# T3 of the down projection from seven inner products, spread among T2, T1 and B22

## The chip, the cores and the metric

The kernel runs on one core of a Trainium2 chip. A core has TensorE (PE, matrix products into PSUM), VectorE (DVE) and ScalarE (ACT) for elementwise work, GpSimd (POOL) and SyncE (SP), which here mostly issue DMAs. Each engine works through its own list of instructions in order, and waits on semaphores for the others. The metric is the device time of one execution in microseconds (us).

## What is computed

```python
x = A_x                                             # 2048 tokens, 640 wide
g = sigmoid((x * gate_w).sum(-1, keepdims=True))
q, k, v = split(x @ wqkv)                           # 32 heads of 20
pq, pk = phi(q), phi(k)                             # phi(t) = where(t > 0, t + 1, exp(t)) + 1e-6
kv, z = einsum("bhsd,bhse->bhde", pk, v), pk.sum over tokens
a = (pq @ kv) / (pq @ z + 1e-6) @ wo
h = sigmoid(x @ w_gate) * (x @ w_up)                # 1536 wide
b = h @ w_down
out = g * a + (1 - g) * b
```

All inputs and the output are float32.

## The kernel before

**Precision.** Each float32 operand is split into a high part (an ACT copy to fp32r) and a low part (a DVE subtraction), by `split`. One product of 128x128 by 128x512 is then three matmuls (`mm3`: high x high, high x low, low x high), written on lines 203 and 205.

**Stages.** The first 300 us or so compute k, the small matrix that k and v make with wo, and q; then twelve steps over the 1536 features compute h, and the attention's scaled pq is prepared on DVE beside them. Both end as rows of one long contraction. The last stage, the down projection, starts near 510 us and contracts this against w_down and the attention's matrix. It is this stage that the change rewrites.

**The down projection.** The 2048 tokens are two pairs (pr = 1 and 0) of two groups of 512 (g0, g1). The contraction has 16 blocks of 128, of which w_down's twelve and the attention's first four form pairs (even, odd), p = 0 to 7; the attention's fifth block is the "rest" (`hr`, `wl`). The output's 640 columns are five blocks of 128; four of them form two pairs (q = 0, 1), the fifth is accumulated apart, in a PSUM tile `rot`. So each pr is a 2x2 by 2x2 block product and is computed by seven products, named B11, B21, T1, T2, T3, T4 and B22 after the form of h that goes in. The forms of h are built by DVE while h is computed, and stored by POOL in DRAM as `h_dram[pr, name]`, one tile of 8 x 512 columns for each (h1T3 is form T3 of pair 1). The weights' forms are E (plain, even blocks), O (plain, odd blocks), SE and SO (sums, built by `load_s` and `sum_s` from line 1510 and kept in `s_dram`), and L for the rest.

A *pass* (class `Pass`) is one form of one pair: four h pieces (pp = 0 to 3), each 128x1024 (two rows of the contraction), against the columns of q = 0, of q = 1 and, in four of the forms, of the fifth block (`EXTRA`). A piece of B11, B21, T1 or B22 thus feeds 18 matmuls, one of T2, T3 or T4 feeds 12. X holds the PSUM sums of B11, T2, T3 and, for pair 0, T4; Z those of T1 and B22; outputs leave through tiles `ot` and stores by POOL (`put`, line 1736).

**What sets the order.** `SEQ` (line 1607) lists the passes: B11 of both pairs piece by piece in turn, B21 of pair 1, T4 of pair 1, B21 of pair 0, then T2, T1, T3 and B22 of pair 1, the same of pair 0, and T4 of pair 0. `HQ` is the list of the h pieces in that order, 56 of them. PE's order follows `HQ`. The h pieces are loaded by SP into raw tiles `hw` (three of them; `load_h`), split by ACT and DVE into tiles `hf` (five of them, `NH`), and used by PE. A split of piece k is queued when piece k - 5 has been used, and the load of piece k + 3 is issued when piece k has been split. Weights come in through two raw tiles `ws` (`load_down`, `next_down`) and are split in the gaps. Where a split stands among ACT's and DVE's other work is decided when the program is built, by class `Order`: it keeps running estimates of each engine's time and takes the next item when it fits (`fill`), at the latest where PE needs it (`need`). `order.late` holds actions that are put into the program when the estimate passes a time.

DMAs of one engine are issued in its program order: where SP waits with a load for data or for a free tile, its later loads wait behind it. The same holds for POOL's stores.

Of the kernel before, what the change touches and what calls it, by code (L numbers as in the profile page):

```python
# [15 lines left out]
P = 128  # L16
# [162 lines left out]
def gated_mix_kernel(ctx: ExitStack, tc: tile.TileContext, xt, xn, wk, wv, wo, wst_q, wst_f, out_t):  # L179
# [81 lines left out]
    s_dram = [dram.tile([P, 2, TG], F32, name=f"s{p}") for p in range(FC // 2 + 2)]  # L261
# [1248 lines left out]
    def load_s(p):  # L1510
        st["in_b"] = not st["q"]
        st["st"] = st["b"][:, 0:2] if st["in_b"] else st["a"][:, 2:4]
        for j in range(2):
            nc.sync.dma_start(st["st"][:, j], raw_down(j, p // 2)[:, p % 2, :4])
        st["s"] = max(order.pe, order.vec) + 6.0

    def sum_s(p):
        e, o = (st["st"][:, j].rearrange("p (o k c) -> p k o c", k=2, c=P) for j in range(2))
        (e0, e1), (o0, o1) = ((t[:, 0], t[:, 1]) for t in (e, o))
# [4 lines left out]
        nc.gpsimd.dma_start(s_dram[p], st["st"])  # L1524
# [14 lines left out]
    hooks = {0: begin, 3: den_all}  # L1539
    NH = 5  # L1540
    WA, RAW = {}, {}

    def wd_tile(key, cols):
        pool = PL["ha"] if key == ("E", 0) else PL["wa"]
# [4 lines left out]
    def load_down(key, t=None):  # L1549
# [3 lines left out]
        if kind == "S":  # L1553
            v = t[:, :8 * P].rearrange("p (j o c) -> p j o c", j=2, c=P)
            nc.sync.dma_start(t[:, :8 * P].rearrange("p (j c) -> p j c", j=2), s_dram[n])
# [3 lines left out]
        else:  # L1559
            src = raw_down(0, n)[:, :, 0::2] if kind == "E" else raw_down(1, n)  # L1560
# [3 lines left out]
        RAW[key] = v, max(order.pe, order.vec) + (8.0 if kind == "S" else 5.0)  # L1564

    d_loads = [("E", pp) for pp in range(1, PP)] + [("O", pp) for pp in range(4)] + [("L", 0)]
    d_loads += [("S", p) for p in range(2 * PP)]

    def next_down():
        if d_loads:  # L1570
            load_down(d_loads.pop(0))

    def queue_down(key):
# [5 lines left out]
        def s_part(j):  # L1579
            t = wd_tile((("SE", "SO")[j], n // 2), 4)  # L1580
            split(t[:, 0, n % 2], t[:, 1, n % 2], RAW[key][0][:, j])
            if j:
                order.then(next_down)

        def diff():
            v = RAW[key][0]
            sub(v[:, KC:], v[:, 0:4:2], v[:, 1:4:2])

        def whole():
            if kind == "L":  # L1590
                t = WA[key] = PL["wa"].tile([P, 2, KC + 2, P], F32R, name="wl", tag="wl")
            else:
                t = wd_tile(key, 3 if kind == "E" else KC)
            split(t[:, 0], t[:, 1], RAW[key][0])
            if key != ("E", 0):
                order.then(next_down)

        if kind == "S":
            for j in range(2):
                order.add(a_cost(4 * P), v_cost(4 * P), lambda j=j: s_part(j), ("wa", ("SE", "SO")[j], n // 2), at)  # L1600
        else:
            w = {"E": 6, "O": 10, "L": 7}[kind] * P
# [4 lines left out]
    SEQ = [[(1, "B11"), (0, "B11")], [(1, "B21")], [(1, "T4")], [(0, "B21")]]  # L1607
    SEQ += [[(pr, n)] for pr in (1, 0) for n in ("T2", "T1", "T3", "B22")] + [[(0, "T4")]]
    HQ = [(pr, n, pp) for turn in SEQ for pp in range(PP) for pr, n in turn]
    HF, HR = {}, {}  # L1610

    def load_h(k, tiles=None):
        if k < len(HQ):
            pr, n, pp = HQ[k]
            if tiles:
                for i, t in enumerate(tiles):
                    nc.sync.dma_start(t, h_dram[pr, n][:, 2 * pp + i])
            else:
                tiles = PL["hb"].tile([P, 2, TG], F32, name="hw", tag="hw", bufs=3)
                nc.sync.dma_start(tiles, h_dram[pr, n][:, 2 * pp:2 * pp + 2])  # L1620
# [17 lines left out]
    REST, REST_AT = {}, {13: 0, 20: 1, 36: 0}  # L1638
# [23 lines left out]
    for f in range(FC):  # L1662
# [36 lines left out]
        if not nxt:  # L1699
            queue_h(0)  # L1700
# [41 lines left out]
    load_h(2)  # L1742
    load_h(3)
    load_h(4)
# [4 lines left out]
    plan += [("S", p) for p in range(2 * PP)]  # L1749
# [4 lines left out]
    hk = done_h = 0  # L1754

    def advance():

        while plan:
# [7 lines left out]
            else:  # L1766
                order.stream = order.mid if kind == "S" else order.items
# [184 lines left out]
```

## Time and profile before

| | us |
|---|---|
| median of 3 runs | 726.71 (726.53 to 726.83) |
| profiled execution | 727.02 |
| its span, from the first to the last instruction | 724.2 |
| PE busy in it | 719.5 |
| DVE, ACT, POOL busy | 486.3, 320.5, 128.9 |

The page gives, for one profiled execution, each engine's busy time, the chain of work that ended last, groups of instructions with their mean time, and the idle time ahead of them with what ended it ("<-ACT hf" means that the engine waited for ACT's work on tile hf). PEld is the weight load, which overlaps the matmuls. Where an action is a DMA, "SPq" or "POOLq" is the queue that issued it. Matmuls overlap too, so a matmul's length is no measure of its place in PE's time; the distance between starts is.

### The profile page before, as it was taken

To read this page: it belongs to the slowest core of one execution; us is meant where nothing else is said; L and a number is where in the kernel's file an instruction comes from. 1 tells how busy PE (TensorE), PEld (TensorE's weight loads), DVE (VectorE), ACT (ScalarE), POOL (GpSimd) and SP (SyncE) were. 2 spreads that over 40 slices of the span, in tenths; PEclk is the share of its full clock that TensorE was granted. 3 is DMA by queue.
4 is the path that set the end of the run, shared out by engine and by line. 5 is a ranking of instruction groups with operands and counts; after the bars stand their busy time and mean duration, and the time that the engine had idled before them with its cause. 6 is when DMAs were issued, how large, how long until landed. Compare 5 with 4: busy or idle time off the path is not lost.

```text
span 724.2 us, 9524 instructions
## 1 busy us (share of the span) xinstructions
PE 719.5 (99%) x3411; PEld 607.8 (84%) x3411; DVE 486.3 (67%) x773; ACT 320.5 (44%) x541; POOL 128.9 (18%) x221
## 2 busy tenths in 40 slices
PE   9999999999999999999999999999999999999997
PEld 8999998888888888888888888888888888888886
DVE  4878576868764698678879778786866664434340
ACT  6664637166756233333333232334367644424321
POOL 0311011122520023213224222330200000010000
PEclk9999999999999999999999999999999999999999
DMA  7553536897555474556578658474987975565431
GB/s 253 140 141 70 162 55 159 201 302 247 191 174 182 153 238 126 176 194 242 188 273 299 221 188 294 157 258 143 324 300 259 329 231 190 158 213 194 146 113 72
DMA packets 59491, 144.05 MB, mean 199 GB/s; under 512 B 7310, under 2 KB 20782, under 8 KB 59445
## 3 DMA queue, kind: packets, MB, share of 16 engines
q1 hardware_dynamic: 40757, 88.50, 38.4%
q0 software_dynamic: 18544, 54.83, 23.2%
q8 instruction: 26, 0.43, 0.3%
q14 instruction: 20, 0.16, 0.1%
q10 hardware_dynamic: 144, 0.13, 0.1%
HBM read 89.81 MB, written 49.84 MB: 193 GB/s over the span
## 4 chain that ended last, share of the span: by engine, by line
PE 99%; DVE 0%; ACT 0%; issue 0%
PE ch L205 18%; PE cc L205 17%; PE rot L205 16%; PE dd L205 14%; PE ch L203 9%; PE cc L203 8%; PE rot L203 8%; PE dd L203 7%; PE cc L1136 1%; PE rot L300 0%; PE cc L1216 0%; DVE ot L219 0%; ACT ot L215 0%
## 5 line engine op out<-in xcount | busy, mean ns | idle before, releaser
L219 DVE TENSOR_TENSOR hf<-hw,hf 128x1024 fp32r<-128x1024 f32 x54 | 65.8, 1223 | 68.7 <-ACT hf L215 68.4
L215 ACT ACTIVATE hf<-hw 128x1024 fp32r<-128x1024 f32 x54 | 56.8, 1057 | 53.7 <-PE rot L205 30.5
L219 DVE TENSOR_TENSOR c<-cc,c 128x512 f32<-128x512 f32 x56 | 37.7, 686 | 45.9 <-PE cc L205 40.5
L205 PE MATMUL dd<-hf,wa 128*128 128x512 f32 x160 | 49.3, 389 | 0.0
L205 PE MATMUL ch<-hf,wa 128*128 128x512 f32 x160 | 49.3, 389 | 0.0
L1736 POOL DMA_DIRECT2D out_t<-ot x18 | 9.7, 540 | 183.8 <-DVE ot L219 180.8
L215 ACT ACTIVATE wG<-wst 128x640 fp32r<-128x640 f32 x17 | 12.4, 737 | 65.0 <-PE dd L205 65.0
L215 ACT ACTIVATE c<-ch 128x512 f32<-128x512 f32 x32 | 19.1, 597 | 48.8 <-PE ch L205 44.0
L205 PE MATMUL rot<-hf,wa 128*128 128x512 f32 x128 | 39.4, 389 | 0.0
L205 PE MATMUL cc<-hf,wa 128*128 128x512 f32 x128 | 39.4, 389 | 0.0
L203 PE MATMUL dd<-xrh,wG 128*128 128x512 f32 x90 | 35.3, 393 | 0.0
L205 PEld LDWEIGHTS ch<-hf,wa 128*128 128x128 f32 x160 | 30.0, 188 | 6.3
L205 PEld LDWEIGHTS dd<-hf,wa 128*128 128x128 f32 x160 | 30.0, 188 | 6.3
L205 PE MATMUL dd<-xrh,wG 128*128 128x512 f32 x90 | 35.1, 390 | 0.0
L205 PE MATMUL dd<-xrl,wG 128*128 128x512 f32 x90 | 35.0, 389 | 0.0
L219 DVE TENSOR_TENSOR c<-c,om 128x512 f32<-128x512 f32 x48 | 33.1, 692 | 1.6
L203 PE MATMUL cc<-xbh,wS 128*128 128x512 f32 x84 | 32.7, 389 | 0.0
L205 PE MATMUL cc<-xbl,wS 128*128 128x512 f32 x84 | 32.7, 389 | 0.0
L205 PE MATMUL cc<-xbh,wS 128*128 128x512 f32 x84 | 32.7, 389 | 0.0
L203 PE MATMUL dd<-hf,wa 128*128 128x512 f32 x80 | 31.1, 389 | 0.0
L203 PE MATMUL ch<-hf,wa 128*128 128x512 f32 x80 | 31.1, 389 | 0.0
L215 ACT ACTIVATE c<-rot 128x512 f32<-128x512 f32 x24 | 14.2, 597 | 38.1 <-PE rot L205 30.8
(471 smaller groups left out, 2084.6 us busy)
## 6 DMA issues: line engine op xcount, KB each, us to landing
hf<-p_dram SPq DMA_DIRECT2D x16, 512.0 KB, 4.7
hw<-h1T SPq DMA_DIRECT2D x16, 512.0 KB, 5.4
hw<-h0T SPq DMA_DIRECT2D x16, 512.0 KB, 4.3
wst<-wst_f SPq DMA_DIRECT2D x12, 640.0 KB, 4.7
xst<-xt SPq DMA_DIRECT2D x10, 640.0 KB, 7.0
h1T<-c POOLq DMA_DIRECT2D x24, 256.0 KB, 2.7
h0T<-c POOLq DMA_DIRECT2D x24, 256.0 KB, 3.0
hw<-h1B SPq DMA_DIRECT2D x11, 512.0 KB, 4.5
```

Of the source, the lines that this page charges most:

```text
L203: nc.tensor.matmul(o, l_hi, r, start=first, stop=False, skip_group_check=True)
L205: nc.tensor.matmul(out, a, b, start=False, stop=last and n == 1, skip_group_check=True)
L215: nc.scalar.activation(out, src, fn, **kw)
L219: nc.vector.tensor_tensor(out, a, b, op=op)
L1136: nc.tensor.matmul(ps[:w, b0:b1], v[:, m, :w], g(m), start=(m == 0), stop=(m == KC - 1))
L1736: (eng or nc.gpsimd).dma_start(out_t[o * P:(o + 1) * P, g * TG + c0:g * TG + c1], t[:, c0:c1])
```

## The change

T3 of both pairs is a product of its own: 2 pairs of tokens, 2 blocks of output columns (q), and a contraction of 8 x 2 blocks (p = 0 to 7, two p in a piece). Before, it is done in full: 2 x 2 x 8 block products of 128x512. After, the contraction is halved too (`KA`: p = 0, 1, 2, 6, `KB`: p = 3, 4, 5, 7), which makes it a 2x2 by 2x2 block product, and it is computed by seven inner products P1 to P7 (class `Inner`), of two pieces each and one output column block.

Sums of T3's forms of h are made by DMAs from DRAM to DRAM that POOL issues: a copy and three adds in turn in `f_sum` (`f_copy`, `f_add`: P7, then P6, then P3 read it at different times), and `f_low`, which adds h0T3's second half onto its first. Unit u = 0 or 1 is the half of these that makes one piece. Sums of the weights (`i_sum`) are made by DVE when they are split (kind "I").

The pieces of P1 to P7 stand among those of T2, T1 and B22 (`mixed`; a "+" is pair 1). P2, P3 and P4 accumulate straight into X. The others go into two PSUM tiles `ch`, are copied by ACT, and added to X by DVE. Since T1 now comes after the last sum into X[1], its output adds X, and T4's output of pair 1 is completed at the end of P2 and P3.

After the last weight load its two raw tiles `ws` join the three `hw` as raw h tiles (`next_h`). The columns of w_down and wo are laid out as blocks 0, 2, 4, 1, 3, so that E's three lie together; E is split in two parts (E: 256 columns, E2: the fifth block).

```diff
+    s_dram = dram.tile([P, FC // 2 + 2, 2 * TG], F32, name="s_dram")
+    f_sum = dram.tile([P, 4, TG], F32, name="f_sum")
...
+    KA, KB = (slice(0, 2), slice(2, 7, 4)), (slice(3, 5), slice(5, 8, 2))
+    KF = (slice(0, 2), slice(2, 4))
+    def f_copy(u):
+        nc.gpsimd.dma_start(f_sum[:, KF[u]], h_dram[1, "T3"][:, KA[u]])
+    def f_add(u, pr, c):
+        nc.gpsimd.dma_start(f_sum[:, KF[u]], h_dram[pr, "T3"][:, c[u]], accum_op=OP.add)
+    def f_low(u):
+        h = h_dram[0, "T3"]
+        nc.gpsimd.dma_start(h[:, KA[u]], h[:, KB[u]], accum_op=OP.add)
...
-    hooks = {0: begin, 3: den_all}
+    hooks = {0: begin, 3: den_all, 5: lambda: f_copy(0), 6: lambda: f_add(0, 0, KA), 11: lambda: f_low(0)}
...
+        elif kind == "I":
+            v = t[:, :8 * P].rearrange("p (b i s c) -> p b i s c", b=2, i=2, c=P)
+            for b, c in enumerate((KA, KB)):
+                nc.sync.dma_start(v[:, b].rearrange("p i s c -> p i (s c)"), s_dram[:, c[n], :2 * P])
...
-            src = raw_down(0, n)[:, :, 0::2] if kind == "E" else raw_down(1, n)
+            src = raw_down(0, n)[:, :, :3] if kind == "E" else raw_down(1, n)
...
-    d_loads += [("S", p) for p in range(2 * PP)]
+    d_loads += [("S", p) for p in range(2 * PP)] + [("I", u) for u in range(2)]
...
             load_down(d_loads.pop(0))
+        else:
+            next_h("ws")
...
+        def i_plain(s):
+            v = RAW[key][0]
+            if s == 0:
+                if n == 0:
+                    WA["I0"] = i_tile("I0")
+                t = WA["I0"]
+                WI["P1", n] = t[:, :, n]
+                split(t[:, 0, n], t[:, 1, n], v[:, 0, :, 0])
+            else:
+                t = i_tile(("I", "E")[n] + str(s))
+                for i, name in enumerate((("P2", "P3"), ("P5", "P7"), ("P4", "P6"))[s - 1]):
+                    WI[name, n] = t[:, :, :, i]
+                split(t[:, 0], t[:, 1], v[:, int(s != 2)])
+            if s == 3:
+                order.then(next_down)
+        def i_sum(s):
+            b11, b12, b21, b22 = (RAW[key][0][:, i // 2, :, i % 2] for i in range(4))
+            if s == 0:
+                sub(b11, b11, b12)
+            elif s == 1:
+                sub(b12, b22, b12)
+            elif s == 2:
+                vec3(b22, b22, -1.0, b11, OP.mult, OP.subtract)
+            else:
+                add(b21, b22, b21)
+        def e_part(c):
+            v = RAW[key][0]
+            t = wd_tile((("E", "E2")[c], n), 2 - c)
+            split(t[:, 0], t[:, 1], v[:, :, 2:] if c else v[:, :, :2])
+            if c and n:
+                order.then(next_down)
...
+            order.add(a_cost(2 * P), v_cost(2 * P), lambda: i_plain(0), ("wa", "I", n), at_i)
+            order.add(a_cost(4 * P), v_cost(4 * P), lambda: i_plain(1), ("wa", "I", n), at_i)
+            for s in range(4):
+                order.add(0, v_cost(2 * P), lambda s=s: i_sum(s), ("wa", "I", n), at_i)
+            for s in (2, 3):
+                order.add(a_cost(4 * P), v_cost(4 * P), lambda s=s: i_plain(s), ("wa", "I", n), at_i)
+        elif kind == "E":
+            for c in range(2):
+                w = (4 - 2 * c) * P
+                order.add(a_cost(w), v_cost(w), lambda c=c: e_part(c), ("wa", ("E", "E2")[c], n), at)
...
+    HQ = [(pr, "B11", pp) for pp in range(PP) for pr in (1, 0)]
+    HQ += whole(1, "B21") + whole(1, "T4") + whole(0, "B21")
+    HQ += mixed("T2+ T2+ P7 T2+ P7 T2+ P1 T2 P1 T2 P6 T2 P6 T2 P5 P5 T1+ P2 T1+ P2 T1+ P3 P3 T1+")
+    HQ += mixed("B22+ P4 B22+ P4 B22+ B22+") + whole(0, "T1") + whole(0, "B22") + whole(0, "T4")
+    INNER = {"P7": (f_sum, KF), "P6": (f_sum, KF), "P3": (f_sum, KF), "P1": (h_dram[1, "T3"], KA),
+             "P2": (h_dram[1, "T3"], KB), "P5": (h_dram[0, "T3"], KA), "P4": (h_dram[0, "T3"], KB)}
...
+    def next_h(tag="hw"):
+        RING.append(tag)
+        load_h(len(RING) - 1)
+    RING = 2 * ["c"]
...
+            if n in INNER:
+                d, c = INNER[n]
+                if (n, pp) in F_DUE:
+                    F_DUE.pop((n, pp))()
+                src = d[:, c[pp]]
+            else:
+                src = h_dram[pr, n][:, 2 * pp:2 * pp + 2]
...
+                if RING[k] == "hw":
+                    tiles = PL["hb"].tile([P, 2, TG], F32, name="hw", tag="hw", bufs=3)
+                else:
+                    tiles = PL["hb"].tile([P, 2 * D], F32, name="ws", tag="ws", bufs=2)[:, :2 * TG].rearrange("p (i c) -> p i c", i=2)
+                nc.sync.dma_start(tiles, src)
...
+            nxt = {"P7": ("P6", 0, KB), "P6": ("P3", 1, KB)}.get(n)
+            if nxt:
+                key = nxt[0], pp
+                F_DUE[key] = lambda: f_add(pp, *nxt[1:])
+                order.late.append((HR[k][1], lambda: F_DUE.pop(key, int)()))
...
-                order.then(lambda: load_h(k + 3))
+                order.then(lambda: next_h(RING[k]))
...
+    REST, REST_AT = {}, {13: 0, 20: 1, 50: 0}
+    F_AT = {20: lambda: f_low(1)}
...
+            f_copy(1)
...
+            f_add(1, 0, KA)
...
-                    C[n, q] = out_tile()
-                    act(C[n, q], ps, AF.Copy, "q")
+                    t = C[n, q] = out_tile()
+                    act(t, ps, AF.Copy, "q")
+                    if n == "T1":
+                        add(t, X[pr][q], C.pop((n, q)), "a")
+                        put(2 * q + 1, self.g1, t)
...
+    class Inner:
...
+        def __init__(self, n):
+            self.n = n
+            if n == "P7":
+                IB["t"] = ps_tile("ch")
+            elif n == "P1":
+                IB["u"] = ps_tile("ch")
+            x = {"P2": (1, 0), "P3": (1, 1), "P4": (0, 0)}.get(n)
+            self.dst = X[x[0]][x[1]] if x else IB["u" if n in ("P1", "P5") else "t"]
+            self.first = n in ("P7", "P1", "P5")
+        def product(self, u, h):
+            w = WI[self.n, u]
+            prod(self.dst, [(w[:, 0, i], w[:, 1, i], h[:, 0, i], h[:, 1, i]) for i in (0, 1)], self.first and u == 0)
+        def out(self):
+            n = self.n
+            if n == "P7":
+                t = PL["ha"].tile([P, 2, 2, 2, P], F32R, name="is", tag="waE0")
+                t = f32(t.rearrange("p a b o c -> p a (b o c)"))
+                IS["P7"], IS["P1"] = t[:, 0], t[:, 1]
+            elif n in ("P6", "P5"):
+                IS[n] = out_tile()
+            elif n in ("P2", "P3"):
+                q = int(n == "P3")
+                t = CS[1].pop(("T4", q))
+                add(t, X[1][q], t, "q")
+                put(2 * q + 1, 2, t)
+            if n in IS:
+                act(IS[n], self.dst, AF.Copy, "q")
+            if n == "P1":
+                add(X[1][0], X[1][0], IS["P1"], "a")
+            elif n == "P6":
+                add(IS["P1"], IS["P6"], IS["P1"], "a")
+                sub(IS["P7"], IS["P1"], IS["P7"])
+                add(X[1][1], X[1][1], IS["P7"])
+            elif n == "P5":
+                add(X[1][1], X[1][1], IS["P5"], "a")
+                add(IS["P5"], IS["P5"], IS["P1"])
+                sub(X[0][0], X[0][0], IS["P1"])
+                sub(X[0][1], X[0][1], IS["P5"])
...
+            if done_h in F_AT:
+                F_AT[done_h]()
+            if done_h == 30:
+                order.need(("r", 1), False)
...
+    def blocks(w):
+        return np.ascontiguousarray(w).reshape(-1, KC, P)[:, [0, 2, 4, 1, 3]].reshape(-1, D)
...
+                      blocks(inputs["B_w_down"]).reshape(FC, P, D)], axis=2)
```

**PE, at the end of T2 of pair 1.** Before, the last piece of T2 of pair 1 (dd is X[1]; wa_5185 its weights) and the first of T1, into ch (Z[1]):

```order
L203 MATMUL dd_4660<-hf_5452,wa_5185 128x512
L205 MATMUL dd_4660<-hf_5452,wa_5185 128x512 x2
L203 MATMUL dd_4660<-hf_5452,wa_5185 128x512
L205 MATMUL dd_4660<-hf_5452,wa_5185 128x512 x2
L203 MATMUL dd_4661<-hf_5452,wa_5185 128x512
L205 MATMUL dd_4661<-hf_5452,wa_5185 128x512 x2
L203 MATMUL dd_4661<-hf_5452,wa_5185 128x512
L205 MATMUL dd_4661<-hf_5452,wa_5185 128x512 x2
L203 MATMUL ch_5376<-hf_5485,wa_4951 128x512
L205 MATMUL ch_5376<-hf_5485,wa_4951 128x512 x2
L203 MATMUL ch_5376<-hf_5485,wa_4951 128x512
L205 MATMUL ch_5376<-hf_5485,wa_4951 128x512 x2
```

After, the last piece of T2 of pair 0 (cc is X[0]) stands there, since T2 of both pairs is over first, and the two pieces of P5 follow, into a ch tile, each with its own weights:

```order
L203 MATMUL cc_4699<-hf_5535,wa_5192 128x512
L205 MATMUL cc_4699<-hf_5535,wa_5192 128x512 x2
L203 MATMUL cc_4699<-hf_5535,wa_5192 128x512
L205 MATMUL cc_4699<-hf_5535,wa_5192 128x512 x2
L203 MATMUL cc_4700<-hf_5535,wa_5192 128x512
L205 MATMUL cc_4700<-hf_5535,wa_5192 128x512 x2
L203 MATMUL cc_4700<-hf_5535,wa_5192 128x512
L205 MATMUL cc_4700<-hf_5535,wa_5192 128x512 x2
L203 MATMUL ch_5472<-hf_5558,wa_5299 128x512
L205 MATMUL ch_5472<-hf_5558,wa_5299 128x512 x2
L203 MATMUL ch_5472<-hf_5558,wa_5299 128x512
L205 MATMUL ch_5472<-hf_5558,wa_5299 128x512 x2
```

A piece of T2 has four products of three matmuls (the x2 row is two of them), a piece of P5 has two: it is used up in half the time.

**SP, the loads around the same place.** Before: the loads of the last two pieces of T2 of pair 1, between the last sums of weights (s6, s7) and T1:

```order
L1555 DMA ws_5122<-s6_97 128x1024
L1620 DMA hw_5144<-h1T2_82 128x1024
L1620 DMA hw_5161<-h1T2_82 128x1024
L1555 DMA ws_5177<-s7_98 128x1024
L1620 DMA hw_5188<-h1T2_82 128x1024
L1620 DMA hw_5232<-h1T1_83 128x1024
L1620 DMA hw_5243<-h1T1_83 128x1024
L1620 DMA hw_5271<-h1T1_83 128x1024
L1644 DMA ot_5298<-r1_100 128x512
L1644 DMA ot_5299<-r1_100 128x512
```

After: the loads from P7's second piece to P6's second. ws is a weight tile for s_dram and a raw h tile where it reads h:

```order
L1725 DMA hw_5238<-f_sum_92 128x1024
L1575 DMA ws_5268<-s_dram_91 128x2x256 x2
L1725 DMA hw_5281<-h1T2_82 128x1024
L1725 DMA ws_5305<-h1T3_84 128x1024
L1725 DMA hw_5324<-h0T2_75 128x1024
L1755 DMA ot_5351<-r1_94 128x512
L1755 DMA ot_5352<-r1_94 128x512
L1725 DMA hw_5360<-h1T3_84 128x2x512
L1725 DMA ws_5390<-h0T2_75 128x1024
L1725 DMA hw_5401<-f_sum_92 128x1024
L1725 DMA ws_5412<-h0T2_75 128x1024
L1725 DMA hw_5424<-f_sum_92 128x1024
```

The inner weights' loads (128x2x256) come where T1's pieces were, two weight tiles take h pieces, and the two loads of f_sum at the end (P6) stand eight rows or more behind the loads of P7, with T2's pieces of both pairs and P1's between them.

**POOL, the stores of the down projection.** Before, the output stores of B21 of both pairs follow one another:

```order
L1736 DMA out_t<-ot_4850 128x512
L1736 DMA out_t<-ot_4863 128x512
L1736 DMA out_t<-ot_5061 128x512
L1736 DMA out_t<-ot_4885 128x512
L1736 DMA out_t<-ot_4898 128x512
```

After, adds stand between them:

```order
L1849 DMA out_t<-ot_4882 128x512
L1849 DMA out_t<-ot_4890 128x512
L1849 DMA out_t<-ot_5094 128x512
L1387 DMA f_sum_92<-h0T3_77 128x1024
L1849 DMA out_t<-ot_4917 128x512
L1387 DMA f_sum_92<-h0T3_77 128x2x512
L1849 DMA out_t<-ot_4930 128x512
L1849 DMA out_t<-ot_5348 128x512
L1391 DMA h0T3_77<-h0T3_77 256x1x512
L1387 DMA f_sum_92<-h1T3_84 128x1024
L1387 DMA f_sum_92<-h1T3_84 128x2x512
L1849 DMA out_t<-ot_5171 128x512
```

The rows of L1387 add h into f_sum: P6's two units, then P3's two. The row of L1391 adds one part of h0T3 onto another, for P5's second piece. A further copy and two adds stand near 500 us among the h stores.

More of the change, by code (lines that the diff above doesn't have):

```diff
@@ L1741, in gated_mix_kernel @@
     PL["hb"] = open_pool("hb")
-    load_h(2)
-    load_h(3)
-    load_h(4)
+    for _ in range(3):
+        next_h()
     next_down()
@@ L1766, in advance @@
             else:
-                order.stream = order.mid if kind == "S" else order.items
+                order.stream = order.mid if kind in "SI" else order.items
                 queue_down((kind, k))
@@ L1884, in close @@
                 put(2 * q + 1, self.g0, t, eng=nc.sync)
[L1886 to L1895 removed]
+    IB, IS = {}, {}
@@ new lines, in gated_mix_kernel @@
+    passes = {}
+    jobs = [(k, q) for k in range(len(HQ) - PP) for q in (0, 1, None)]
+    jobs += [(k, q) for q in (0, 1, None) for k in range(len(HQ) - PP, len(HQ))]
+    for k, q in jobs:
+        pr, n, pp = HQ[k]
+        if (pr, n) not in passes:
+            passes[pr, n] = Inner(n) if n in INNER else Pass(pr, n)
+        b = passes[pr, n]
+        order.need(("h", k))
+        if n in INNER:
+            if q is None:
+                order.need(("wa", "I", pp))
+                b.product(pp, HF[k])
+                if pp == 1:
+                    b.out()
+        else:
```

118 lines of the change are left out of this document (59 added, 59 removed).

## The prediction

> **What bounds the kernel now.** I read the page's busy table and chain first, then the windows by stage, to see whether any stage waits.
>
> ```profile
> span 724.2 us, 9524 instructions
> PE 719.5 (99%) x3411; PEld 607.8 (84%) x3411; DVE 486.3 (67%) x773; ACT 320.5 (44%) x541; POOL 128.9 (18%) x221
> PEclk9999999999999999999999999999999999999999
> PE 99%; DVE 0%; ACT 0%; issue 0%
> 400.00:500.00 100.00, 100.00 (x443) 82.81 (x442) 77.73 (x132) 31.69 (x56) 26.48 (x49) 1.00 0.59 209
> 500.00:600.00 100.00, 100.00 (x443) 82.81 (x442) 69.08 (x83) 54.95 (x73) 9.70 (x18) 1.00 0.84 286
> 600.00:724.20 124.20, 120.39 (x535) 99.60 (x533) 44.60 (x45) 39.91 (x47) 6.47 (x12) 1.00 0.47 151
> ...
> 0.85 3.32 PE rot L300 x9
> ...
> 720.94 0.34 SPq L1736 DMA_DIRECT2D out_t<-ot  x1
> ```
>
> The span is 724.2 us, PE is busy for 719.5 of it and the chain is PE from end to end. The windows (columns: PE, PEld, DVE, ACT, POOL busy, clock, DMA share, GB/s) say that this holds stage by stage: both full hundreds carry 443 matmuls, before the down projection and in it. The clock is full. What is not PE is 0.85 us ahead of the first matmul and, at the end, about 3.9 us of last copies and a store that is issued at 720.94; the change touches neither. So a matmul taken out is worth its full place in the row, as long as nothing new makes PE wait.
>
> What one place is worth comes from the spacing of PE's timeline, not from the matmul's own 389 ns, since neighbours overlap:
>
> ```profile
> 510.76 0.39 PE L203 MATMUL dd<-hf,wa 128*128 128x512 f32 x1
> 535.24 0.39 PE L203 MATMUL dd<-hf,wa 128*128 128x512 f32 x1
> 592.36 0.39 PE L203 MATMUL dd<-hf,wa 128*128 128x512 f32 x1
> ```
>
> The first row opens h piece 0, the second h piece 6. Each of the six B11 pieces between has 18 matmuls, so 24.48 us hold 108: **0.2267 us each**. The third row opens piece 20, the first of T2 of pair 1, where the order of the work begins to differ.
>
> **The change, part by part.** *Matmuls.* T3 was 2 pairs x 4 pieces x 2 outputs x 2 rows x 3 = 96 matmuls. The seven inner products are 7 x 2 pieces x 2 rows x 3 = 84. Nothing else on PE changes in number: 12 x 0.2267 = **-2.72 us**, all on the path.
>
> *Splits.* The down projection goes from 56 h pieces to 62, since an inner piece feeds only 6 matmuls where a T3 piece fed 12. Each piece costs one load, one ACT and one DVE pass:
>
> ```profile
> L219 DVE TENSOR_TENSOR hf<-hw,hf 128x1024 fp32r<-128x1024 f32 x54 | 65.8, 1223 | 68.7 <-ACT hf L215 68.4
> L215 ACT ACTIVATE hf<-hw 128x1024 fp32r<-128x1024 f32 x54 | 56.8, 1057 | 53.7 <-PE rot L205 30.5
> hw<-h1T SPq DMA_DIRECT2D x16, 512.0 KB, 5.4
> 542.70 0.42 DVE L219 TENSOR_TENSOR ws<-ws 128x256 f32<-128x256 f32 x1
> 498.76 0.68 DVE L219 TENSOR_TENSOR c<-c,c 128x512 f32<-128x512 f32 x1
> 515.17 0.95 DVE L219 TENSOR_TENSOR wa<-ws,wa 128x768 fp32r<-128x768 f32 x1
> 602.14 0.60 ACT L215 ACTIVATE ot<-dd 128x512 f32<-128x512 f32 x1 [3.08 <-PE dd L205]
> ```
>
> Pieces 20 to 43 (T2 of both pairs, T1 of pair 1, ten inner pieces) hold 48 + 48 + 72 + 60 matmuls and 6 for the fifth chunk: 234 x 0.2267 = 53.0 us for 24 pieces, 2.2 us a piece. DVE needs 24 x 1.22 = 29.4 us of it, about 4.2 us for the second set of inner weights (four 0.42 us sums, then splits of 0.42 and three of 0.68), 8 x 0.68 = 5.4 us for new sums into PSUM, and a few output adds: near 42 of 53. ACT needs less. Neither is the bound, so I cost this at nothing; the cover is PE's own 53 us. Were the cover gone, the extra DVE work of the change, some 17 us with the six pieces, would be the price.
>
> *Weights.* The first E pass is split in two, which puts one instruction's overhead (0.68 and 0.42 where a 128x768 took 0.95) on DVE ahead of piece 2, 0.15 us. E's columns now lie together, so its loads go in longer rows. The bound is 0.15 us lost, or nothing; the margin below hides it. The smaller S splits pay for most of the inner weights on ACT.
>
> *DMA between DRAM and DRAM.* Two plain copies, and eight adds: two before 500 us (f_add, f_low of unit 0), one near 502 (f_add of unit 1), and five from about 584 to 618 (two that turn P7's sum into P6's, f_low of unit 1, two that turn P6's into P3's). The trace has no DRAM-to-DRAM add. The nearest rows are adds of 320 KB into SBUF (zacc), in windows in which nothing else moves, and a DRAM-to-DRAM copy (180 to 184):
>
> ```profile
> 96.00:99.00 3.00, 3.00 (x23) 3.00 (x22) 3.00 (x5) 0.00 (x0) 0.37 (x1) 1.00 0.62 109
> 60.00:64.00 4.00, 4.00 (x23) 3.57 (x22) 3.27 (x6) 1.68 (x3) 0.23 (x1) 1.00 0.51 82
> 178.28 1.11 POOL L1164 DMA_DIRECT2D mp_dram<-m_dram  x2 [4.47 <-DMA m_dram<-ms]
> 180.00:184.00 4.00, 4.00 (x20) 3.30 (x19) 2.52 (x3) 3.01 (x5) 2.97 (x6) 1.00 0.97 352
> 488.00:500.00 12.00, 12.00 (x55) 9.94 (x54) 6.05 (x9) 4.17 (x7) 0.00 (x0) 1.00 0.32 119
> 504.00:528.00 24.00, 24.00 (x108) 19.87 (x107) 18.52 (x26) 10.10 (x13) 5.38 (x10) 1.00 0.99 341
> 592.00:622.00 30.00, 30.00 (x134) 24.86 (x133) 11.52 (x11) 12.95 (x16) 1.08 (x2) 1.00 0.60 193
> 596.00:600.00 4.00, 4.00 (x19) 3.34 (x18) 2.13 (x2) 1.40 (x2) 0.00 (x0) 1.00 1.01 393
> ```
>
> 327 KB of adding took 0.62 x 3 = 1.86 us of all DMA engines, or 0.51 x 4 = 2.04 us in the form with shorter rows: about half the rate of a copy. For 512 KB that is 2.98 to 3.26 us. From the other side an add that cost no more than a copy is 512 KB at 352 GB/s and 0.97, 1.45 us; one that pays double for having both ends in DRAM is 6.0. I take 2.98, the row nearest in shape (h's rows are longer still); 1.45 and 6.0 stay for the range. The adds and copies before 500 us fall where the engines are 0.32 busy, and cost nothing.
>
> *Near 502 us* the engines are 0.99 busy for 24 us, so f_add puts off what is queued by up to 2.98. Who would notice:
>
> ```profile
> 510.76 0.85 ACT L215 ACTIVATE wa<-ws 128x768 fp32r<-128x768 f32 x1 [2.37 <-DMA ws<-wst_f]
> 516.04 2.36 DVE L219 TENSOR_TENSOR hf<-hw,hf 128x1024 fp32r<-128x1024 f32 x2
> 529.70 1.22 DVE L219 TENSOR_TENSOR hf<-hw,hf 128x1024 fp32r<-128x1024 f32 x1
> ```
>
> ACT waits for E's load until 510.76. Its product and piece 2 are used by PE from 510.76 + 36 x 0.2267 = 518.9. Going back from there, DVE must start on piece 2 by 517.7 (1.22), and before that ACT makes two passes over E (about 1.0) and one over piece 2 (1.06): the load may land as late as 515.6, 4.8 us of room. Piece 6 is split at 530.9 and used at 535.24: 4.3 us. Both exceed 2.98, so nothing.
>
> *From 592 to 622 us* (pieces 20 to 33) is the tightest place. What must move there for PE not to wait at piece 36: pieces 28 to 36, 9 x 1.52 us (512 KB at 341 GB/s, 0.99) = 13.7; five transfers of 256 KB (three stores, two rest loads) at 0.76 = 3.8; four adds x 2.98 = 11.9 (the fifth, P6's first, falls before 592). That is 29.4 of 30 us, where 0.60 x 30 = 18 were used before; at the 393 GB/s of 596 to 600 it is 27.4. It fits, barely. The two old weight buffers that join the h ring make ten pieces in flight, about 20 us from issue to use against a landing of 5.4. Hence again nothing, with a very thin cover.
>
> *New waits.* SP must hold P6's loads until POOL's add has landed, and every later h load queues behind on SP. P7's load stands eight pieces, some 17 us, ahead of P6's; landing (5.4) and an add of about 4 come to under 10. P3's loads stand ten and eleven pieces behind P6's. On PE, T1 of pair 1 takes over the PSUM tile of P5 as its second output: ACT copies it after two h splits, and PE reaches it 6 matmuls (1.36 us) later, against 0.60 for the copy and what is left of a 1.06 us split. Between nothing and 0.5 us; I take nothing.
>
> **Sum.** -2.72, no new wait: span 721.5. The profiled execution took 727.02 us, 2.8 above its span, and the median shown is 726.71; -2.72 from the median gives **724.0 us**.
>
> **Rivals.** *A: the transfers of 592 to 622 don't fit, and the result is slower.* Beyond the point where an add costs 3.1 us (loads at 341 GB/s) to 3.6 (at 393), each further microsecond of an add is four of PE wait, near pieces 34 to 36 where a piece lasts only 1.36 us. At 3.6 with slow loads the stall is 1.9 us (725.9, within 0.2%). At 4.25 or more the stall passes 4.2, and the kernel is slower: 4.5 us per add gives 724.0 + 5.5 = 729.5, 6.0 gives 735.5. For it: 99% filling by my own sum, and an add never seen in DRAM. Against it: the copy at 352 GB/s, which reads and writes DRAM, shows no penalty for having both ends there.
>
> *D: DRAM itself is the limit, not the 16 engines.* An add passes DRAM three times (two reads, a write), 1.57 MB. Four adds, nine loads and five small transfers are 6.3 + 4.7 + 1.3 = 12.3 MB; if the 393 GB/s of the fastest window were all that DRAM gives, they would take 31.3 us and PE would wait 1.3: 725.3. Against it: the copy's 352 GB/s is 704 through DRAM, so 393 is no ceiling. The Trainium skill ("DMA: Bandwidth & Descriptors", Specifications) gives a core about 358 GB/s of HBM, by which the same 12.3 MB take 34.4 us and the estimate is 724.0 + 4.4 = 728.4, slower. By that rule the change gives back more than it takes; the trace doesn't agree with it, by the same 704 and 393.
>
> *B: the full stretch from 504 to 528 gives way.* If the add there costs 6.0 and each piece behind it is late by that, piece 6 is 6.0 - 4.3 = 1.7 us late: 725.7. It decides from 4.3 us per add. Against it: E's loads now go in longer rows, and an add would have to cost twice what it cost into SBUF.
>
> *C: small handovers in PSUM and behind late ACT passes* cost 0.3 to 1.2 us together: 724.3 to 725.2.
>
> **How the numbers follow.** This kernel's runs lie within 0.3 us of each other, so 0.2% (1.45 us) is about what a measurement can tell from no change: faster is below 725.26, slower above 728.16. Forecast as worked out, 723.6 to 724.5: 0.53. C: 0.10. A in its mild form, 725.3 to 728.1: 0.10, for its cover is under 1 us; B 0.07; D 0.04, since a row speaks straight against it. A beyond 4.25 us per add, 728.2 and up: 0.16. So faster 0.63, same 0.21, slower 0.16. Below 723.6 nothing leads, since the tail and the other matmuls stay. To leave out no more than 2 in 10 the range must go to 728.0; the forecast's own is 723.6 to 724.5.
>
> **What would show it.** Right: PE has 12 matmuls fewer, its timeline has no gap behind 510 us, and the last output store stands 2.7 us earlier. Wrong by A: a gap at pieces 28 to 36, ended by an h split whose ACT pass waited for its load, with the DMA share near 1.0 from 585 to 622 and an add landing late. Wrong by B: a gap between 515 and 545, ended by a wa or hf split. Wrong by C: gaps under 1 us, ended by ACT or DVE at ch or dd.

## The result, and the profile after

The changed kernel took **731.25 us** (median of six runs, 730.6 to 732.2), the kernel before on the same chip 726.62 us (726.37 to 726.83): a ratio of 1.0064, 95% interval 1.0051 to 1.0077. It is slower by 4.6 us, where 724.0 was forecast and 728.0 was the top of the range. The profiled execution took 732.2 us, 1.7 above its span.

The page's head, its busy table and its chain, and the windows by stage (columns: PE, PEld, DVE, ACT and POOL busy, clock, DMA share, GB/s):

```profile
span 730.5 us, 9634 instructions
PE 719.8 (99%) x3399; PEld 605.8 (83%) x3399; DVE 504.1 (69%) x807; ACT 330.9 (45%) x563; POOL 139.3 (19%) x231
PE 86%; DMA 6%; DVE 3%; ACT 3%; issue 1%; SPq 0%; DVEq 0%; ACTq 0%
400.00:500.00 100.00, 100.00 (x443) 82.84 (x442) 77.57 (x135) 32.88 (x59) 27.96 (x51) 1.00 0.68 231
500.00:600.00 100.00, 100.00 (x443) 82.84 (x442) 74.25 (x102) 56.18 (x85) 14.18 (x22) 1.00 0.88 286
600.00:730.50 130.50, 122.59 (x535) 99.22 (x533) 59.73 (x62) 49.63 (x60) 8.60 (x14) 0.99 0.60 191
```

The busy table has 12 matmuls fewer, as worked out. The chain is what changed: it was 99% PE, and now 6% of it is DMA, 3% DVE and 3% ACT, so PE waits. Both full hundreds still hold 443 matmuls each; the loss behind the start of the down projection lies past 600 us. The waits of PE (engine, tile and line, what it waited for, us in total, times, longest) name the places; a line of three dots stands for rows left out:

```profile
PE cc L1137 <- ACT gtb L215: 1.7, 1, 1.7
PE ch L205 <- DVE hf L219: 1.6, 2, 0.8
PE dd L205 <- DVE hr L219: 0.9, 1, 0.9
...
PE dd L203 <- ACT hr L215: 0.8, 1, 0.8
PE ch L203 <- ACT hf L215: 0.4, 1, 0.4
PE cc L205 <- DVE hf L219: 0.3, 1, 0.3
PE ch L203 <- ACT ot L215: 0.2, 1, 0.2
```

A wait is shorter than the hole that it makes in the row of matmuls, since neighbours overlap. So I measured the holes: the spacing of PE's starts beyond 0.2267 us for each matmul. There are three groups. Between 614 and 634 us the holes add up to **3.98 us**; they end in splits of h, all but the last 0.5 us, which end when ACT has copied P5's sum out of PSUM (ot). Near 691 us they are **2.31 us**, and end in splits of hr, the rest of pair 0. The third, 2.75 us, lies ahead of the down projection (its first matmul starts at 513.51, before at 510.76), with 1.75 of them in the wait for gtb near 158 us. -2.72 + 3.98 + 2.31 + 2.75 = +6.32, which is the difference of the spans, 730.5 - 724.2 = 6.3.

What released PE in the first group, from the chain of waits (start, us, what):

```profile
598.72 10.67 DMA hw<-h1T
609.65 0.78 issue
...
613.90 1.06 ACT hf L215
614.98 1.24 DVE hf L219
616.24 11.28 DMA hw<-h0T
627.60 1.06 ACT hf L215
```

Two loads of an h piece (pieces 28 and 35) took 10.7 and 11.3 us from issue to landing, where the median before was 5.4. The windows there:

```profile
590.00:600.00 10.00, 10.00 (x46) 8.29 (x45) 8.49 (x15) 5.96 (x10) 4.00 (x5) 1.00 1.02 287
600.00:610.00 10.00, 10.00 (x46) 8.29 (x45) 4.58 (x5) 4.44 (x6) 0.00 (x0) 1.00 1.06 296
610.00:620.00 10.00, 9.74 (x44) 7.73 (x43) 8.67 (x9) 8.28 (x12) 1.99 (x2) 1.00 1.02 272
620.00:630.00 10.00, 8.04 (x33) 5.66 (x31) 4.55 (x6) 3.94 (x6) 0.00 (x0) 1.00 1.01 328
```

The DMA engines are full for 40 us while PE (the first pair of numbers) falls to 8.04 of 10. That is what rival A said would show it wrong. The second group is something that no rival named. ACT's rows there:

```profile
684.38 1.06 ACT L215 ACTIVATE hf<-ws 128x1024 fp32r<-128x1024 f32 x1 [3.02 <-PE rot L205]
688.47 1.06 ACT L215 ACTIVATE hf<-hw 128x1024 fp32r<-128x1024 f32 x1 [3.02 <-PE rot L205]
689.43 1.13 ACT L215 ACTIVATE hr<-ot 128x512 fp32r<-128x512 f32 x2
```

The passes over hr stand behind two splits of h, and each of these had to wait until PE left an hf buffer. When ACT reaches hr at 689.43, PE needs it 0.2 us later. Before, ACT made the same hr at 662.68, and PE used it first at 674.6:

```profile
662.68 1.14 ACT L215 ACTIVATE hr<-ot 128x512 fp32r<-128x512 f32 x2
L203 PE MATMUL dd<-hr,wl x4: 389/389/389, 674.6 to 705.2; 128*128 128x512 f32 x4
```

Its load was issued 27.6 us ahead of that use there (at 647.00), and 16.8 us ahead of the need here (at 672.82); it landed in 5.5 and 5.1 us.

### The profile page after: what moved, and what is told of

The parts are those of the page before. It is cut to its first block, busy times and chain, and to the rows that moved or that the text cites. A ratio compares the mean times of both kernels' runs of the same rounds, so it can differ in the third digit from the quotient of the medians.

```text
span 730.5 us, 9634 instructions
## 1 busy us (share of the span) xinstructions
PE 719.8 (99%) x3399; PEld 605.8 (83%) x3399; DVE 504.1 (69%) x807; ACT 330.9 (45%) x563; POOL 139.3 (19%) x231
## 3 DMA queue, kind: packets, MB, share of 16 engines
HBM read 98.20 MB, written 55.08 MB: 210 GB/s over the span
## 4 chain that ended last, share of the span: by engine, by line
PE 86%; DMA 6%; DVE 3%; ACT 3%; issue 1%; SPq 0%; DVEq 0%; ACTq 0%
PE ch L205 17%; PE rot L205 15%; PE cc L205 14%; PE dd L205 11%; PE ch L203 8%; PE rot L203 7%; PE cc L203 7%; PE dd L203 5%; DMA hw<-h0T 2%; DMA hw<-h1T 1%; ACT hf L215 1%; DMA wo_sb<-wo 1%; DMA xst<-xt 1%; DMA zacc<-kb 1%; PE rot L301 1%
## 5 line engine op out<-in xcount | busy, mean ns | idle before, releaser
L219 DVE TENSOR_TENSOR hf<-hw,hf 128x1024 fp32r<-128x1024 f32 x45 | 54.7, 1223 | 29.9 <-ACT hf L215 29.5
L205 PE MATMUL ch<-hf,wa 128*128 128x512 f32 x192 | 59.3, 390 | 1.6 <-DVE hf L219 1.6
L215 ACT ACTIVATE hf<-hw 128x1024 fp32r<-128x1024 f32 x45 | 47.2, 1056 | 29.0 <-PE rot L205 20.6
L205 PE MATMUL dd<-hf,wa 128*128 128x512 f32 x144 | 44.3, 389 | 0.0
L205 PEld LDWEIGHTS ch<-hf,wa 128*128 128x128 f32 x192 | 35.8, 188 | 9.6 <-DVE hf L219 2.2
L203 PE MATMUL ch<-hf,wa 128*128 128x512 f32 x96 | 37.7, 393 | 0.6 <-ACT hf L215 0.4
L219 DVE TENSOR_TENSOR hf<-ws,hf 128x1024 fp32r<-128x1024 f32 x15 | 18.3, 1223 | 23.2 <-ACT hf L215 23.1
L205 PE MATMUL cc<-hf,wa 128*128 128x512 f32 x104 | 32.1, 390 | 0.3 <-DVE hf L219 0.3
L205 PEld LDWEIGHTS dd<-hf,wa 128*128 128x128 f32 x144 | 27.0, 188 | 5.6
```

The costliest lines, as they stand in the source:

```text
L203: nc.tensor.matmul(o, l_hi, r, start=first, stop=False, skip_group_check=True)
L205: nc.tensor.matmul(out, a, b, start=False, stop=last and n == 1, skip_group_check=True)
L215: nc.scalar.activation(out, src, fn, **kw)
L219: nc.vector.tensor_tensor(out, a, b, op=op)
```

## The experiments

All ran beside the kernel before, whose medians were 726.60, 726.45 and 726.62 us in the three sets. "Holes" is the sum measured as above from 600 to 640 us in the profile of each run.

**1. The rest's place in ACT's queue.**

```
-... (8.0 if done_h < 13 else 11.0)
+... (8.0 if done_h < 13 else 6.0 if done_h == 50 else 11.0)
```

> The changed kernel with the split of the second rest (hr for pair 0) due 6 us instead of 11 us after its load is issued; the load itself stays where it is. In the profile of the changed kernel PE waits 2.3 us near 690 us for hr, and ACT makes hr right behind a split of h that had to wait until PE left an hf buffer. Theory of the queue's order: hr stands ahead of two splits of h now, the 2.3 us go, 731.25 becomes 728.9. Rival, that the rest's load lands late: the stall stays, 731.2.

727.53 us, ratio 1.0011 (1.0002 to 1.0021). ACT's rows:

```profile
678.62 1.06 ACT L215 ACTIVATE hf<-hw 128x1024 fp32r<-128x1024 f32 x1 [2.53 <-PE rot L205]
679.59 1.14 ACT L215 ACTIVATE hr<-ot 128x512 fp32r<-128x512 f32 x2
```

The load is where it was, hr is made before the two splits of h and not behind them, and the holes near 690 us are gone; those from 600 to 640 stay (4.20 us). So it was the order of the queue and not a late load. The median is 3.7 us below the first one of the changed kernel and 2.8 below its second (experiment 5), more than the 2.3 that were worked out.

**2 to 4. The five adds: their transfers or their waits.** One run leaves them out, one lets them go where nothing waits for them, one keeps the waits and shrinks the transfers.

```
# without the adds
-    F_AT = {20: lambda: f_low(1)}
+    F_AT = {}
-            nxt = {"P7": ("P6", 0, KB), "P6": ("P3", 1, KB)}.get(n)
+            nxt = None
# no waits: the same 512 KB each, into h tiles of B11
+        d, at = SPARE.pop(0)
+        nc.gpsimd.dma_start(d[:, at:at + 2], h_dram[pr, "T3"][:, src], accum_op=OP.add)
# small: the tight five move 64 of 512 columns
+        w = 64 if c is KB else TG
+        nc.gpsimd.dma_start(f_sum[:, KF[u], :w], h_dram[pr, "T3"][:, c[u], :w], accum_op=OP.add)
```

> The changed kernel without the five adds of the tight stretch (P6 twice, P3 twice, f_low of unit 1), so P6, P3 and half of P5 get wrong inputs. PE's gaps from 614 to 633 us add up to 4.0 us. If the adds are their cause (by their transfers or by the waits they bring), the gaps go and 731.25 becomes 727.3; if PSUM handovers, more splits or the planner's order are, they stay, 731.2.

> The five adds are kept with their 512 KB each, but they add into h tiles of B11 that nobody reads any more, so nothing waits for them and they wait for no load of an inner piece (P6, P3 and half of P5 get wrong inputs). If the transfers themselves are too much for the DMA engines, most of the 4.0 us stays: 729.7 to 731.3. If it is the waits (SP held behind an add, POOL held behind a load), the gaps go: 727.3.

> The five adds keep all their waits and places but move 64 of 512 columns (P6, P3 and half of P5 get wrong inputs). If the transfers are too much, at most 1 us of the 4.0 us stays: 727.3 to 728.3. If the waits are the cause, 3 us or more stay: 730.2 to 731.3.

Without adds 726.1 us (ratio 1.0004, 0.9982 to 1.0026) and no hole from 600 to 640. With the transfers but without the waits 731.36 us (1.0060, 1.0045 to 1.0075) and holes of 3.96. With the waits but an eighth of the transfers 726.87 us (1.0005, 0.9985 to 1.0026) and none. The adds are the cause, by what they move; SP held behind an add, or POOL behind a load, isn't needed for it. The second run isn't the same stall in every detail: since nothing holds its adds back, one of them is issued at 564 us and four between 591 and 596, where the changed kernel issues P3's two at 612.9 and 615.6, and its holes lie between 610 and 620 us. It shows that the transfers alone can cost 4 us.

What else moved there is seen best without the adds, in the same 30 us of the program that the prediction summed up (592 to 622; 0.36 later here, as the down projection starts 0.36 later). The window, and the issues in it with their count and median time to landing:

```profile
592.36:622.36 30.00, 30.00 (x134) 24.86 (x133) 20.92 (x26) 19.08 (x27) 1.09 (x2) 1.00 0.81 270
hw<-h1T SPq DMA_DIRECT2D x3, 512.0 KB, 5.6
ws<-h0T SPq DMA_DIRECT2D x3, 512.0 KB, 5.5
hw<-f_sum SPq DMA_DIRECT2D x2, 512.0 KB, 5.8
hw<-h0T SPq DMA_DIRECT2D x2, 512.0 KB, 4.6
ws<-h1T SPq DMA_DIRECT2D x2, 512.0 KB, 6.3
ot<-r SPq DMA_DIRECT2D x2, 256.0 KB, 5.7
out_t<-ot POOLq DMA_DIRECT2D x2, 256.0 KB, 5.7
```

Twelve h loads are issued, not nine, and with what was under way at the edges 0.81 x 30 = 24.3 us of all DMA engines are taken before any add.

What an add costs comes from the queue of POOL (packets, MB, share of 16 engines), 580 to 632 us, with the five adds (first row, experiment 1) and without (second row, experiment 2):

```profile
q0 software_dynamic: 1344, 3.41, 35.7%
q0 software_dynamic: 240, 0.79, 3.9%
```

(0.357 - 0.039) x 52 = 16.5 us for five adds, **3.3 us each** on average. This is engine time while other transfers are in flight; no run has such an add by itself.

**5. The changed kernel again**, because of the 2.75 us at the start:

> The changed kernel once more, unaltered, beside the others on one chip. Its first profile lost 2.75 us before the down projection began, 1.75 of them in one wait near 158 us that the four profiles since do not have. If that belongs to single executions, this one begins the down projection at 511 to 512 us (before: 510.76) and takes 2.3 us more than the kernel with the earlier split of the rest: 729.8. If it belongs to the change (the placement of its tensors), the wait is there again: 731.3.

730.31 us, 1.0055 (1.0040 to 1.0070). The wait near 158 us isn't there, nor in the profile of any other experiment, and the down projection starts at 511.58. That wait was one of the first profile only.

By the same sum this profile has 4.40 us of holes from 600 to 640, but 1.7 of them are no wait. From 627.8 to 631.2, right behind the waits, PE's starts are 0.43 us apart instead of 0.2267, and the clock that the profile shows as granted is 0.5; it lowers the mean of these two windows (the third number from the right):

```profile
620.00:630.00 10.00, 8.44 (x31) 6.16 (x30) 6.59 (x7) 6.42 (x9) 0.00 (x0) 0.89 0.95 320
630.00:640.00 10.00, 10.00 (x43) 8.25 (x42) 8.48 (x10) 4.77 (x6) 0.00 (x0) 0.94 0.84 286
```

The profiles of experiments 3 and 4 have such a stretch of 3.4 us too, right behind the holes at hr (from 690.2 and from 687.1 us); the first profile of the changed kernel has the holes and no such stretch.

**6 and 7. Fewer adds in the tight stretch**, both with the earlier split of the rest. The first issues f_low of unit 1 after piece 8, which leaves four adds; the second also makes P6's sum of unit 0 ahead, which leaves three:

```
-    F_AT = {20: lambda: f_low(1)}
+    F_AT = {9: lambda: f_low(1)}
# and for the second
-    f_sum = dram.tile([P, 4, TG], F32, name="f_sum")
+    f_sum = dram.tile([P, 6, TG], F32, name="f_sum")
+    def f_ahead(add):
+        if add:
+            nc.gpsimd.dma_start(f_sum[:, 4:6], h_dram[0, "T3"][:, KB[0]], accum_op=OP.add)
+        else:
+            nc.gpsimd.dma_start(f_sum[:, 4:6], f_sum[:, KF[0]])
-    hooks = {... 11: lambda: f_low(0)}
+    hooks = {... 8: lambda: f_ahead(False), 11: lambda: (f_low(0), f_ahead(True))}
```

> The earlier split of the rest (727.5 by itself), and f_low of unit 1 issued after piece 8 (near 545 us) instead of piece 19 (near 597 us), so that four adds and not five move in the tight stretch. If PE's gaps of 4.0 us are an excess of transfers, 3.5 us of DMA time less leaves 0.5 to 1.5 us: 724.0 to 725.0. If the excess sits in the P6 and P3 adds alone (single loads stuck behind them), the gaps stay: 727.5.

> As the one before, and P6's sum of unit 0 is made near 491 us in columns of f_sum of its own (one more plain copy near 440 us), so three adds are left in the tight stretch. If it is an excess of transfers, no gap is left from 600 to 640 us: 723.4 to 724.0. If an add more near 491 us delays the loads of E (room of 4.8 us worked out in the prediction), a gap of up to 3 us appears between 513 and 520 us: up to 726.5.

With four adds 726.42 us (1.0004, 0.9991 to 1.0016) and holes of 3.45, much more than I expected to be left, and nearer to the other outcome that was put down, that the gaps stay. With three **724.47 us** (0.9972, 0.9963 to 0.9982) and no hole anywhere behind 500 us: this version is 2.0 us (0.3%) faster than the kernel before.

Why one add less helped so little, in windows of the run with four:

```profile
604.00:608.00 4.00, 4.00 (x19) 3.33 (x18) 0.51 (x2) 1.91 (x3) 0.00 (x0) 1.00 1.02 410
608.00:612.00 4.00, 4.00 (x20) 3.30 (x19) 3.44 (x4) 4.00 (x7) 0.88 (x1) 1.00 0.63 202
612.00:616.00 4.00, 4.00 (x19) 3.32 (x18) 3.79 (x4) 3.50 (x5) 1.17 (x1) 1.00 0.98 161
616.00:620.00 4.00, 4.00 (x19) 3.32 (x18) 1.44 (x2) 0.00 (x0) 0.00 (x0) 1.00 0.97 226
```

From 608 to 612 us the DMA engines stand idle for a third: SP's rows show no h load between 604.32 and 609.04, since no raw buffer is free. Then both adds for P3 start (609.83 and 612.38) together with six h loads. Room that is made ahead of such a burst can't be stored; this reading rests on the windows, and no run tried it by itself. Experiment 12 fits it: it leaves out one of these two adds as well, and the holes fall by another 2.6 us, where f_low, taken out from ahead of the burst, gave 0.75. But the run with three adds (experiment 7) had the same burst at the same time and no holes, and its bytes went faster (245 GB/s from 612 to 616, against 161). It also differs in f_sum, whose rows lie 12 KB apart there instead of 8.

**8. Both stalls taken out**, by the earlier split and without the five adds:

> The earlier split of the rest, and the five adds of the tight stretch left out (P6, P3 and half of P5 get wrong inputs). Both stalls are gone then, and what is left is the forecast's sum: 12 matmul places, 2.72 us, less than before, a span of 721.5 to 722.0 and 723.4 to 724.2 in all. If more splits, PSUM handovers or late ACT passes cost something by themselves, it is above 724.5.

723.72 us (0.9981, 0.9955 to 1.0007), span 722.3, no hole behind 500 us. Its down projection starts at 511.68, 0.92 later than in the profile of before, and 724.2 - 2.72 + 0.92 = 722.4: the matmul term is right to 0.2 us. The medians say the same: 726.45 - 723.72 = 2.73 us.

**9 to 12. The number of adds, or the distance of f_sum's rows.**

```
# 9 (four adds) and 10 (five adds): two columns of f_sum are never used
-    f_sum = dram.tile([P, 4, TG], F32, name="f_sum")
+    f_sum = dram.tile([P, 6, TG], F32, name="f_sum")
# 11: the version with P6 ahead, rows 16 KB apart
+    f_sum = dram.tile([P, 8, TG], F32, name="f_sum")
# 12: four adds less one, rows 8 KB apart
-            if nxt:
+            if nxt and (n, pp) != ("P6", 0):
```

> f_low of unit 1 early and the earlier split of the rest, as in the kernel that took 726.4 with gaps of 3.1 us left, and f_sum declared with six columns of which two are never used, so that its rows are 12 KB apart and not 8. The kernel with P6's sum ahead had three adds and rows 12 KB apart; this one has four adds. If the number of adds decides, the gaps stay at 3 us: 726.4. If the distance of f_sum's rows decides, they go: 723.5 to 724.5.

> The changed kernel with only the earlier split of the rest (727.5, gaps of 4.1 us) and f_sum's rows 12 KB apart, five adds in the tight stretch. If the number of adds decides: 727.5. If the distance of the rows decides, the gaps fall under 2 us: 725.5 or less.

> The kernel with P6's sum of unit 0 ahead (724.5, three adds, no gaps) with f_sum's rows 16 KB apart instead of 12. If the number of adds decides: 724.5, no gaps. If rows at a power of two apart are what slows an add: gaps of 2 us or more, 726.5.

> f_low of unit 1 early and the earlier split of the rest, and P3's add of unit 0 left out (P3 gets a wrong input), so that three adds are left with f_sum's rows 8 KB apart, and one instead of two at 610 us. If the number of adds decides: no gaps, 723.4 to 724.5. If the distance of the rows decides: gaps of 2 us or more, 726.

Two of these expectations give the holes of earlier runs as 3.1 and 4.1 us; by the sum used here they are 3.45 and 4.20. All runs with the earlier split of the rest, together:

| adds in the stretch | f_sum's rows apart | holes 600 to 640, us | median, us | ratio (95%) |
|---|---|---|---|---|
| 5 | 8 KB | 4.20 | 727.53 | 1.0011 (1.0002 to 1.0021) |
| 5 | 12 KB | 2.75 | 725.88 | 0.9995 (0.9979 to 1.0010) |
| 4 | 8 KB | 3.45 | 726.42 | 1.0004 (0.9991 to 1.0016) |
| 4 | 12 KB | 1.40 | 724.99 | 0.9985 (0.9964 to 1.0006) |
| 3 | 8 KB | 0.86 | 723.97 | 0.9964 (0.9951 to 0.9977) |
| 3 | 12 KB | 0 | 724.47 | 0.9972 (0.9963 to 0.9982) |
| 3 | 16 KB | 0 | 724.80 | 0.9975 (0.9965 to 0.9984) |
| 0 | 8 KB | 0 | 723.72 | 0.9981 (0.9955 to 1.0007) |

Both count; neither theory alone was right. At either distance the holes shrink with every add taken out, to under 1 us at three; with three adds it also differs which of them is gone. At the same number of adds, wider rows take off another 0.9 to 2.0 us. POOL's queue with five adds and rows 12 KB apart, to set beside the 35.7% above, then with four adds and rows 8 KB and 12 KB apart, and with three adds and rows 8 KB and 12 KB apart:

```profile
q0 software_dynamic: 1344, 3.41, 32.7%
q0 software_dynamic: 1072, 2.88, 30.7%
q0 software_dynamic: 1072, 2.88, 27.1%
q0 software_dynamic: 928, 2.36, 25.3%
q0 software_dynamic: 928, 2.36, 21.3%
```

(0.327 - 0.039) x 52 / 5 = 3.0 us per add instead of 3.3, for the same packets and bytes. One of the five is f_low, whose destination is a tile of h with rows 16 KB apart in every run. With four or three adds all go into f_sum, and the price is 3.5 and 3.7 us with rows 8 KB apart against 3.0 and 3.0 with 12 KB. In the run with rows 16 KB apart a hole of 0.86 us appears near 558 us instead, at the rest of pair 1; I did not follow it.

## Why the prediction was wrong

**The matmul term was right.** -2.72 us is what is left when both stalls are out (experiment 8).

**The step that failed is the sum for 592 to 622 us**: "That is 29.4 of 30 us ... It fits, barely." The price of an add was not far off: 2.98 us was taken from adds into SBUF, and 3.3 were measured (3.0 with wider rows). What was mis-sized is the rest of the sum. I counted the loads that piece 36 needs, nine, and five small transfers, 17.5 us; experiment 2 shows 24.3. The ring of five raw buffers sends a load whenever a buffer comes free, so the loads of pieces 37 to 39 move in the same 30 us, and they share the engines with the ones that are needed first. With four adds at 3.3 us that is 37.5 us of work for 30, and at the predicted 2.98 it would have been 36.2. The prediction held numbers that would have told it. It counted ten inner pieces among pieces 20 to 43; there are twelve, so these 24 pieces hold 246 matmuls and not 234, and 55.8 us of PE and not 53.0. They need 24 x 1.52 = 36.5 us of loads, five adds of 3.3 need 16.5, and the five transfers of 256 KB 3.8: 56.8 us for 55.8. That the ring's early loads are what makes the needed ones late is read from the windows; no run held the ring back.

**Rival A was the mechanism**, at the pieces and with the signs that it named. A first hole of 0.5 us stands at piece 29, the others at pieces 34 to 36. Its price was not right: by its own formula a 3.3 us add would have cost 0.7 us, since it started from the same 17.5. The waits were 4.0 and 2.7 us in the two profiles of the changed kernel and 4.2 in that of experiment 1, and not 4 us for each microsecond beyond a threshold: 37.5 - 30 = 7.5, of which the rest is work for later pieces that could come late. Three adds of 3.0 still make 24.3 + 9.0 = 33.3 us for 30, and that kernel had no hole. So such a sum tells that loads come late, and not by how much; what sets the size of the stall stays open.

**A step was left out altogether.** The change moves the second rest from 36 pieces to 50. The prediction counted rest loads only as transfers, and never asked where the split of hr lands in ACT's queue. That cost 2.3 us, half of what the kernel lost. No trace of before could show it, but the order of ACT's rows in the changed program could: hr stands there behind two splits of h whose buffers PE frees last.

**Near 502 us nothing happened**, as worked out and against rival B: no hole from 505 to 600 us in either profile of the changed kernel. **New waits on SP and the PSUM handovers (rival C)** cost nothing by themselves: with an eighth of the transfers and all waits kept, no hole is left from 600 to 640 us, though small adds also make the waits behind them shorter. The 0.5 us at P5's copy come only behind late loads. **Rival D** is not told apart from A, since both put the limit at the same transfers. Its flat ceiling of 393 GB/s falls: 415 moved in this stretch of the best version. The third pass of an add through DRAM, which D counted, isn't seen in the totals of the profile pages: five adds more (the changed kernel against experiment 2) make 98.20 - 95.58 MB of reads and 55.08 - 52.46 MB of writes, one of each per add.

```profile
620.00:624.00 4.00, 4.00 (x20) 3.30 (x19) 2.97 (x4) 3.67 (x6) 0.00 (x0) 1.00 1.03 415
```

The Trainium skill ("Perfetto Trace Analysis", Roofline) says that 358 GB/s is a core's share when both cores of a pair draw on the memory, and puts the ceiling of a single core at about 435, set by its 16 DMA engines; the 415 agree with that, and by that page the 358 that the prediction weighed is no ceiling for a kernel on one core.

**The median.** The medians differ by 731.25 - 726.62 = 4.63 us, and by 730.31 - 726.45 = 3.86 in the repeat. -2.72 + 2.31 + about 4.0 gives 3.6. The rest, 1.0 and 0.3 us, is open. The later start of the down projection is no sign of a cost of the change: it lies between 510.96 and 511.75 us in the profiles of the twelve experiments and at 510.76 in the one profile of before, but that execution, with its span of 724.2 us, was near the shortest. The runs of the kernel before that were made beside the experiments have median spans of 724.9, 724.6 and 724.6 us (nearly all lie between 724.1 and 725.8), and experiment 8 lies 2.73 us below the median beside it, which leaves nothing for a later start. One contribution to the rest may be the clock: three of the six runs of the changed kernel have a mean granted clock of 0.997 or 0.998, and a stretch like that of experiment 5 costs 1.7 us; of the 78 runs of the kernel before beside the experiments, one is below 0.999. Only profiled runs show where the clock fell.

## What to carry to other kernels

When a change trades matmuls for transfers, sum up all that moves in the stage by what the stage consumes (pieces times the cost of a load, plus what is new), not by what the next wait needs: a ring that runs ahead also moves, in the same time, loads that nobody needs yet. Move the added transfers out to where the engines are idle, one by one, and look whether they still meet in one burst. And when a load is moved, look up where the instruction that uses it now stands in its engine's queue, and what the one ahead of it waits for.

## What was not expected of the hardware

An add of 512 KB between two places in DRAM took 3.5 to 3.7 us of all DMA engines when the rows of its destination lay 8 KB apart (experiments 6 and 12), and 3.0 us with rows 12 KB apart (experiments 7, 9 and 10); the run with three adds did about as well at 16 KB as at 12, so it isn't the power of two as such. The medians, each taken against the kernel before beside it, fell by 1.67 us (five adds) and 1.60 us (four adds) from two columns that are never used. Why 8 KB is worse was not settled. A larger f_sum may also move the tensors that are laid out behind it in DRAM, and no run tells the two apart.

Behind a stall of 2 to 3 us PE can run at half its clock for 3.4 us, which costs another 1.7: three of the profiles show it, at 627.8, 690.2 and 687.1 us. It doesn't follow every such stall.
